# A hand-ordered attention and two feed-forward layers on one core: the order remade with VectorE and GpSimd taking turns, run on to unit fourteen, and constant matmuls ahead of the first load

## The chip, the cores and the metric

The kernel runs on one core of a Trainium2 chip. The metric is the device time of one execution in microseconds (us). The engines are TensorE (PE; its weight loads are PEld), VectorE (DVE), ScalarE (ACT), GpSimd (POOL) and SyncE (SP), on whose queue all the DMAs named below are issued.

## The reference

Three layers follow one another. All tensors are float32.

```python
# attention: q, k, v are (4, 8, 576, 64)
q_rot, k_rot = rotate(q), rotate(k)          # pairs (d, d+32) turned by position
scores = scale * q_rot @ k_rot^T
attn   = exp(scores - rowmax);  attn /= rowsum + 1e-9
x      = (attn @ v) -> (2304, 512)
# layer 2: w_in (512, 2048), w_out (2048, 512)
h = maximum(x @ w_in, 0);  x = h * h @ w_out
# layer 3: 8 experts, w1 (8, 512, 1024), w2 (8, 1024, 512)
e = argmax(x @ w_gate + modality_bias[modality_id])
out[t] = gate[t] * (maximum(x[t] @ w1[e], 0) @ w2[e])
```

## The kernel before

**Precision.** Matmul operands are split into a high part (rounded to the matmul's format) and a low part (the rest). A product is three passes: high by high, high by low, low by high.

**Attention** goes in 16 chunks of two heads. For a chunk, raw q and k (128 x 2 x 576: the values and their swapped partners) are loaded (`ldq`, `ldk`), multiplied by tables (`aq`, `bq`, `ak`, `bk`) and added (`cq`, `ck`; all L206). Then come the cast of the high part (`qh`, `kh`), the low part (`ql`, `kl0`, `kl1`; L195), and copies of both to the other partitions (`qd0` to `qd2`, `kd0` to `kd2`), by an engine or by DMA. There are nine groups of score rows; for each, matmuls into one of two PSUM buffers (`sc0` to `sc8`, L266), the maximum on VectorE (`mx`, L271), and the exponential on ScalarE, which also gives the row sums (`ex`, L282). TensorE transposes the exponentials (`trm..`, `trr.`; L324), an engine copies them out (`evm..`, `evr.`), and TensorE multiplies them by v (`pv0`, `pv1`). `sa` (the guard, L290) adds 1e-9 to the nine sums of a partition, `srec` takes the reciprocals, `sev` and `rst` send them to memory; `u0`, `u1` take the products out of PSUM. For the first four chunks `xn`, `xh`, `xl` normalise and split the result.

**The first block of layer 2.** A unit is one 128-wide slice f of the 2048 hidden columns for 512 tokens: `m1f` (12 matmuls of 512 columns, L649), `re`, `sq`, `gg`, `gl` (ScalarE and VectorE make the square and split it), `m2f` (12 matmuls of 512 columns, L685). Weights come as 32 chunks of 512 KB: `m1f` needs chunk 2f, `m2f` needs chunk 2f+1. A chunk goes through `wd` (load, into one of four raw buffers, L467), `wx` (ScalarE, L476 and L477), `wy` (VectorE, L481 and L482), `wz` (GpSimd, L486), `wb` (VectorE, L490; this frees the raw buffer), `wh` (ScalarE, L504) and `wl` (VectorE or GpSimd, L507). From chunk 10 on, `wh` needs memory that attention gives back. Later blocks of tokens use the converted weights again.

**The order** is written out: `ORDER` (L38) is a string of words `chunk.name.engine`, with V VectorE, A ScalarE, P GpSimd, T TensorE and D a DMA on SP's queue. Chunk 16 stands for the first block. The words are issued in this order; each engine runs its own in order, and semaphores keep what depends on one another. `HQ` (L436) is the number of units that are in `ORDER` whole. From unit `HQ` on a loop (L1087) issues the rest in program order: `m1` of two units ahead, what is listed for the unit (`at`, L1007), then `m2`. Before, with 12, the last words of the order make `m113` and `m211`, and the loop begins with `m114`, `m212`, `m115`, `m213`, `m116`. `m116` is the first of the next block of tokens and needs its x: `xk` and `xw` load reciprocals and values, `xnorm` multiplies, `xsplit` splits.

Of the kernel before, what the change touches and what calls it, by code (L numbers as in the profile page):

```python
# [43 lines left out]
1.kl0.P 0.trrk.T 0.ex8.A 0.evrk.V 0.evm02.V 1.kl1.P 1.sc1.T 1.sc3.T 0.evm00.A 0.evm03.A 1.mx1.V 1.ex1.A 1.mx3.V
0.trm13.T 1.ex3.A 0.sa.P 0.trm12.T 16.wx0.A 1.sc2.T 0.srec.V 0.evm13.V 0.evm12.V 0.trrr.T 0.trm11.T 1.mx2.V 2.ldq.D
1.ex2.A 1.sc0.T 1.qd2.D 0.trm10.T 1.sc6.T 0.evrr.A 1.mx0.V 2.ldk.D 1.ex0.A 0.evm11.A 1.sc5.T 2.aq.P 2.bq.P 0.trm01.T
1.trm02.T 2.cq.V 2.ak.V 2.bk.P 1.mx6.V 1.mx5.V 2.qh.A 0.sev.A 2.ck.V 2.ql.V 1.ex6.A 2.qd0.D 3.ldq.D 1.evm02.A
0.evm01.V 2.kh.A 1.ex5.A 2.kd1.A 1.trm03.T 1.sc8.T 2.kl0.P 1.mx8.V 2.kd0.V 1.ex8.A 2.qd1.D 0.trrq.T 0.evm10.V 0.evrq.A
2.kl1.P 1.trm00.T 1.sc4.T 1.sc7.T 1.mx7.V 2.kd2.D 0.rst.D 16.wy0.V 3.ldk.D 2.qd2.D 1.ex7.A 0.pv0.T 1.mx4.V 1.ex4.A
1.evm03.V 2.sc2.T 1.sa.V 2.mx2.V 3.aq.P 3.bq.P 1.srec.V 1.evm00.A 0.u0.A 2.ex2.A 1.trrq.T 2.sc1.T 3.cq.V 3.ak.V 3.bk.P  # L50
1.trm01.T 1.trm12.T 2.sc3.T 0.pv1.T 3.qh.A 1.evm01.A 2.mx1.V 2.mx3.V 3.ck.V 2.ex1.A 3.ql.V 2.ex3.A 0.rld.D 3.qd0.D
2.sc7.T 1.evrq.V 4.ldq.D 16.wz0.P 2.sc6.T 1.trm10.T 1.evm12.A 3.kh.A 1.trm11.T 3.kd1.A 2.mx7.V 2.mx6.V 3.kl0.P 2.ex7.A
2.sc4.T 1.trrr.T 2.ex6.A 3.kd0.V 2.sc0.T 3.qd1.D 1.evm11.A 0.u1.A 2.mx4.V 2.ex4.A 1.trm13.T 2.mx0.V 2.ex0.A 1.trrk.T
3.kl1.P 3.kd2.D 2.sc5.T 4.aq.V 1.evm10.A 2.sc8.T 1.evrr.A 2.mx5.V 0.xr.D 2.trm01.T 1.evm13.V 4.bq.P 2.mx8.V 3.qd2.D
1.sev.V 4.ldk.D 2.ex5.A 4.cq.P 2.evm01.A 2.ex8.A 3.sc2.T 2.trm13.T 3.mx2.V 4.qh.V 2.trm12.T 2.evm13.V 2.trm02.T
3.ex2.A 3.sc1.T 1.evrk.A 2.sa.P 2.evm02.A 3.sc3.T 3.mx1.V 4.qd0.D 2.trrq.T 2.trm11.T 3.mx3.V 2.trm00.T 3.ex1.A
2.evm12.V 2.evm11.V 4.ql.P 2.srec.V 2.ldv.D 4.bk.P 3.ex3.A 3.sc7.T 5.ldq.D 4.ak.P 2.trrk.T 3.sc6.T 2.evrq.A 2.trrr.T
3.mx7.V 16.wb0.V 4.ck.P 3.mx6.V 2.evrk.A 1.pv1.T 3.ex7.A 16.wx1.A 4.kh.V 2.evrr.V 3.sc4.T 3.ex6.A 1.u1.A 3.sc0.T
1.pv0.T 4.kd1.D 3.mx4.V 16.wx4.A 4.qd2.D 3.ex4.A 4.kd0.A 3.mx0.V 3.ex0.A 0.xn.P 4.kl0.V 3.sc5.T 5.aq.V 3.sc8.T 0.xh.A
4.kl1.V 3.mx5.V 1.u0.V 4.kd2.D 3.trm01.T 4.qd1.A 5.bq.P 3.mx8.V 2.trm10.T 5.ldk.D 3.ex5.A 2.sev.A 5.cq.P 2.evm00.V  # L60
3.evm01.A 3.ex8.A 2.evm10.A 4.sc3.T 2.trm03.T 3.trm13.T 5.qh.V 4.mx3.V 4.sc2.T 3.trm12.T 4.ex3.A 3.evm13.V 3.trm02.T
2.evm03.A 4.sc1.T 3.sa.P 3.evm02.A 1.rst.D 5.qd0.D 3.trrq.T 3.trm11.T 4.mx2.V 3.trm00.T 3.evm12.V 4.mx1.V 3.evm11.V
5.ql.P 3.srec.V 3.ldv.D 1.rld.D 5.bk.P 4.ex2.A 2.rst.D 6.ldq.D 5.ak.P 4.ex1.A 3.trrk.T 4.sc0.T 3.evrq.A 3.trrr.T
16.wy4.V 4.sc4.T 2.pv1.T 5.ck.P 4.mx0.V 4.mx4.V 4.ex0.A 3.evrk.A 4.ex4.A 5.kh.V 3.evrr.V 0.xl.V 5.kd1.D 0.xst.D
5.qd2.D 5.kd0.A 16.wh0.A 4.sc5.T 5.kl0.V 4.sc6.T 4.mx5.V 4.mx6.V 2.pv0.T 4.ex5.A 6.aq.V 5.kl1.V 4.ex6.A 5.kd2.D 2.u0.A
5.qd1.A 4.sc7.T 6.bq.P 4.ldv.D 3.trm10.T 6.ldk.D 1.xn.V 3.sev.A 6.cq.P 2.rld.D 4.sc8.T 3.evm00.V 4.mx7.V 2.u1.V
4.trm00.T 3.evm10.A 4.trm01.T 4.ex7.A 4.evm00.A 5.sc3.T 16.wy1.V 4.mx8.V 4.trm13.T 3.trm03.T 4.trm10.T 6.qh.V
4.evm01.A 16.wz4.P 4.trrk.T 5.mx3.V 4.ex8.A 5.sc2.T 4.evm13.V 5.ex3.A 3.evm03.A 4.trm12.T 4.evrk.A 5.sc1.T 4.trrq.T
4.trm11.T 6.qd0.D 4.evm10.V 5.mx2.V 4.sa.V 5.mx1.V 4.srec.V 4.trm03.T 6.ql.P 4.evm12.A 6.bk.P 4.trm02.T 5.ex2.A
4.evrq.A 3.rst.D 7.ldq.D 6.ak.P 5.ex1.A 4.evm02.A 4.evm11.V 4.trrr.T 5.sc0.T 1.xh.A 16.wd2.D 4.evm03.V 5.sc4.T 3.pv1.T  # L70
4.evrr.V 1.xl.V 6.ck.P 5.mx0.V 1.xst.D 5.mx4.V 16.wb4.V 5.ex0.A 16.wx2.A 5.ex4.A 6.kh.V 2.xn.V 4.sev.V 4.pv1.T 2.xr.D
2.xh.A 6.kd1.D 6.qd2.D 2.xl.V 6.kd0.A 5.sc5.T 6.kl0.V 5.sc6.T 5.mx5.V 5.mx6.V 2.xst.D 3.pv0.T 1.xr.D 5.ex5.A 4.pv0.T
7.aq.V 16.wy2.V 6.kl1.V 5.ex6.A 6.kd2.D 4.u1.A 3.u0.A 6.qd1.A 5.sc7.T 7.bq.P 5.ldv.D 4.rst.D 4.u0.A 7.ldk.D 7.cq.P
# [5 lines left out]
6.sc6.T 6.mx5.V 6.mx6.V 3.xst.D 6.ex5.A 5.pv0.T 8.aq.V 7.kl1.V 6.ex6.A 7.kd2.D 5.u1.A 7.qd1.A 6.sc7.T 8.bq.P 6.ldv.D
5.rst.D 5.u0.A 8.ldk.D 8.cq.P 6.sc8.T 6.mx7.V 6.trm00.T 16.wd3.D 5.xr.D 6.trm01.T 6.ex7.A 6.evm00.A 7.sc3.T 6.mx8.V  # L80
6.trm13.T 6.trm10.T 8.qh.V 6.evm01.A 6.trrk.T 7.mx3.V 6.ex8.A 7.sc2.T 6.evm13.V 7.ex3.A 6.trm12.T 6.evrk.A 7.sc1.T
6.trrq.T 6.trm11.T 8.qd0.D 6.evm10.V 7.mx2.V 6.sa.V 7.mx1.V 6.srec.V 6.trm03.T 8.ql.P 6.evm12.A 8.bk.P 6.trm02.T
7.ex2.A 6.evrq.A 9.ldq.D 8.ak.P 7.ex1.A 6.evm02.A 6.evm11.V 6.trrr.T 7.sc0.T 6.evm03.V 7.sc4.T 6.evrr.V 8.ck.P 7.mx0.V
7.mx4.V 7.ex0.A 7.ex4.A 16.wz2.P 8.kh.V 6.sev.V 6.pv1.T 8.kd1.D 16.wb2.V 8.qd2.D 8.kd0.A 7.sc5.T 8.kl0.V 7.sc6.T
7.mx5.V 7.mx6.V 16.wd5.D 7.ex5.A 6.pv0.T 9.aq.V 16.wx6.A 8.kl1.V 7.ex6.A 8.kd2.D 6.u1.A 8.qd1.A 7.sc7.T 9.bq.P
16.wy6.V 7.ldv.D 6.rst.D 6.u0.A 9.ldk.D 9.cq.P 7.sc8.T 7.mx7.V 7.trm00.T 6.xr.D 7.trm01.T 7.ex7.A 7.evm00.A 8.sc3.T
7.mx8.V 7.trm13.T 7.trm10.T 9.qh.V 7.evm01.A 7.trrk.T 8.mx3.V 7.ex8.A 8.sc2.T 7.evm13.V 8.ex3.A 7.trm12.T 7.evrk.A
8.sc1.T 7.trrq.T 7.trm11.T 9.qd0.D 7.evm10.V 8.mx2.V 7.sa.V 8.mx1.V 7.srec.V 7.trm03.T 9.ql.P 7.evm12.A 9.bk.P
7.trm02.T 16.wl4.P 8.ex2.A 7.evrq.A 10.ldq.D 9.ak.P 8.ex1.A 7.evm02.A 7.evm11.V 7.trrr.T 8.sc0.T 7.evm03.V 8.sc4.T
7.evrr.V 9.ck.P 8.mx0.V 8.mx4.V 8.ex0.A 8.ex4.A 9.kh.V 7.sev.V 7.pv1.T 16.wx5.A 9.kd1.D 9.qd2.D 9.kd0.A 16.wh2.A  # L90
8.sc5.T 9.kl0.V 8.sc6.T 8.mx5.V 8.mx6.V 8.ex5.A 7.pv0.T 10.aq.V 9.kl1.V 8.ex6.A 9.kd2.D 16.wy5.V 7.u1.A 9.qd1.A
8.sc7.T 10.bq.P 8.ldv.D 7.rst.D 7.u0.A 10.ldk.D 10.cq.P 8.sc8.T 8.mx7.V 8.trm00.T 7.xr.D 8.trm01.T 8.ex7.A 8.evm00.A
9.sc3.T 8.mx8.V 8.trm13.T 8.trm10.T 10.qh.V 8.evm01.A 8.trrk.T 9.mx3.V 8.ex8.A 9.sc2.T 8.evm13.V 9.ex3.A 8.trm12.T
# [1136 lines left out]
```

## Time and profile before

| | |
|---|---|
| median of 3 runs | 951.85 us (950.51 to 952.6) |
| profiled execution | 952.28 us, span 950.5 us |
| mean granted TensorE clock | 0.987 |
| TensorE busy | 894.2 us (94%) |
| VectorE, ScalarE, GpSimd busy | 649.4 (68%), 483.9 (51%), 263.1 (28%) |
| DMA | 117.28 MB, mean 123 GB/s |

The profiled execution's time is a little longer than its span, which goes from the first to the last instruction. Busy shares are means over stages of different kinds: attention ends near 299 us, the first block of layer 2 near 390 us, and what follows is mostly matmul. In the table of stretches below, the columns behind the length are PE, PEld, DVE, ACT and POOL (busy us and instructions), the granted TensorE clock, the DMA engines' busy share and GB/s; in the views of instructions, what stands in brackets is the engine's idle time before and what ended it.

### The profile page before, as it was taken

What the parts mean: (1) busy time and instruction counts of PE and PEld (TensorE: products, weight loads), DVE (VectorE), ACT (ScalarE), POOL (GpSimd) and SP (SyncE); (2) the same over time, 40 slices, a digit from 0 to 9 for tenths busy, and PEclk for the clock granted to TensorE, in tenths of its full rate; (3) what the DMA queues carried; (4) which work ended last, traced back from release to release, by engine and by line L of the source; (5) the groups of instructions that cost most, each with busy time, mean ns of one, the idle gap of its engine ahead of it and who ended that gap; (6) DMA issues with size and microseconds to landing.
All of it is one profiled execution on the core that took longest, in us unless ns stands there. A gap on an engine that the chain in (4) does not pass through costs nothing. (4 is left out here: it accounts for less than half of the span.)

```text
span 950.5 us, 14463 instructions
## 1 busy us (share of the span) xinstructions
PE 894.2 (94%) x5210; PEld 749.3 (79%) x5210; DVE 649.4 (68%) x1213; ACT 483.9 (51%) x956; POOL 263.1 (28%) x201
## 2 busy tenths in 40 slices
...
GB/s 230 136 129 159 175 207 146 154 164 156 190 125 204 122 128 83 163 123 12 1 54 80 1 1 72 17 1 1 45 200 45 111 214 269 227 215 237 204 101 35
DMA packets 47856, 117.28 MB, mean 123 GB/s; under 512 B 10448, under 2 KB 14560, under 8 KB 47776
## 3 DMA queue, kind: packets, MB, share of 16 engines
...
q14 instruction: 37, 0.30, 0.1%
HBM read 92.56 MB, written 15.54 MB: 114 GB/s over the span
## 5 line engine op out<-in xcount | busy, mean ns | idle before, releaser
L655 ACT ACTIVATE r<-h 128x512 f32<-128x512 f32 (+1 forms) x80 | 44.3, 554 | 230.8 <-PE h L649 214.8
L649 PE MATMUL h<-xs,w 128*128 128x512 f32 (+1 forms) x660 | 144.1, 368 | 1.2 <-DVE gl L667 1.2
L663 DVE SCALAR_TENSOR_TENSOR h<-h,r 128x512 f32<-128x512 f32 (+1 forms) x80 | 51.5, 643 | 124.9 <-ACT r L655 124.7
L685 PE MATMUL y<-w,gh 128*128 128x512 f32 x396 | 124.6, 396 | 11.1 <-ACT w L504 11.1
L649 PEld LDWEIGHTS h<-xs,w 128*128 128x128 f32 x660 | 115.8, 188 | 23.2 <-DVE gl L667 2.0
L282 ACT ACTIVATE e<-sc,nmx 128x576 f32<-128x576 f32 x144 | 106.4, 741 | 50.3 <-DVE nmx L271 48.9
L266 PE MATMUL sc<-kh,q 128*128 128x288 f32 (+1 forms) x336 | 100.0, 335 | 32.1 <-ACT e L282 18.7
L271 DVE TENSOR_REDUCE nmx<-sc 128x1 f32<-128x576 f32 x144 | 105.6, 752 | 17.8 <-PE sc L266 15.6
L266 PEld LDWEIGHTS sc<-kh,q 128*128 128x128 f32 x336 | 63.7, 199 | 52.5 <-ACT e L282 34.2
L923 DVE TENSOR_TENSOR w<-eraw,w 128x1024 fp32r<-128x1024 f32 x64 | 78.4, 1225 | 33.9 <-ACT w L922 33.5
L685 PEld LDWEIGHTS y<-w,gh 128*128 128x128 f32 x396 | 74.4, 191 | 26.6 <-ACT w L504 11.5
L266 PE MATMUL sc<-kl,q 128*128 128x288 f32 (+2 forms) x336 | 91.5, 308 | 0.0
L324 PE MATMUL b<-ident,e 128*128 128x128 f32 x640 | 82.9, 277 | 1.4 <-DVE et L192 0.8
L685 PE MATMUL y<-w,gl 128*128 128x512 f32 x198 | 78.0, 394 | 0.4 <-DVE gl L667 0.4
L969 PEld LDWEIGHTS h<-ye,w 128*128 128x128 f32 x576 | 74.0, 189 | 3.7
L324 PEld LDWEIGHTS b<-ident,e 128*128 128x128 f32 x640 | 74.4, 142 | 2.5 <-DVE et L192 1.1
L969 PE MATMUL h<-ye,w 128*128 128x256 f32 x576 | 74.8, 280 | 0.0
L992 PE MATMUL y<-w,ge 128*128 128x512 f32 x288 | 74.7, 395 | 0.0
L570 POOL TENSOR_TENSOR xraw<-xraw,rbs 128x512 f32<-128x512 f32 (+1 forms) x14 | 16.6, 1189 | 203.9 <-DMA rbs<-rD 189.6
L922 ACT ACTIVATE w<-eraw 128x1024 fp32r<-128x1024 f32 x64 | 67.3, 1052 | 4.1 <-DMA eraw<-wexp 4.1
L353 PE MATMUL b<-et,v 128*64 128x288 f32 x512 | 69.0, 412 | 0.0
L697 DVE SCALAR_TENSOR_TENSOR junk<-ysb,wgb 128x512 f32<-128x512 f32 x96 | 64.3, 725 | 0.0
(225 smaller groups left out, 1650.9 us busy)
## 6 DMA issues: line engine op xcount, KB each, us to landing
...
```

Source lines behind the costliest of these rows:

```text
L266: nc.tensor.matmul(out=o[:, x:x + w], lhsT=q[:, hd, q0:q0 + 128], rhs=k[:, hd, y:y + w], start=(n == 0), stop=(n == len(ops) - 1))
L271: nc.vector.tensor_reduce(out=m, in_=sc(p, j)[:, :, 0:HS], axis=AX.XY, op=ALU.max, negate=True)
L282: nc.scalar.activation(out=e(p)[:, o:o + S].rearrange("p (a b) -> p a b", a=2), in_=sc(p, j)[:, :, 0:HS], func=ACTF.Exp, bias=live[p, f"nm ...
L324: nc.tensor.transpose(t[:, i * 128:(i + 1) * 128], x[:, o:o + 128], ident)
L353: nc.tensor.matmul(out=o[64 * hd:64 * hd + 64], lhsT=lhsT, rhs=rhs, start=(c == 0), stop=(c == 4))
L649: nc.tensor.matmul(out=h, lhsT=w[:, a, k * 128:(k + 1) * 128], rhs=xs[b, k][:, c], start=(k == 0 and i == 0), stop=(k == 3 and i == 2))
L685: nc.tensor.matmul(out=yp[t], lhsT=g[a][:, t * 128:(t + 1) * 128], rhs=w[:, c, 512:1024], start=(begin and i == 0), stop=(f == NFC - 1 and ...
L697: nc.vector.scalar_tensor_tensor(out=junk, in0=ysb[j], scalar=1.0, in1=wgb[e], op0=ALU.mult, op1=ALU.mult, accum_out=lg[:, j, e:e + 1])
L922: nc.scalar.activation(out=w[:, 0], in_=r, func=ACTF.Copy)
L923: nc.vector.tensor_tensor(out=w[:, 1], in0=r, in1=f32(w[:, 0]), op=ALU.subtract)
L969: nc.tensor.matmul(out=h, lhsT=w[:, a, k * 128:(k + 1) * 128], rhs=x[:, c], start=(k == 0 and i == 0), stop=(k == 3 and i == 2))
L992: nc.tensor.matmul(out=yp[s, t], lhsT=g[a][:, t * 128:(t + 1) * 128], rhs=w[:, c, 512:1024], start=(f == 0 and i == 0), stop=(f == EFC - 1 ...
```

## The change

- `ORDER` is another string. It holds the same words for chunks 0 to 15, in another order and with other engines for many of them; the 16 guards, of which 13 were VectorE's, are all GpSimd's.
- `HQ` goes from 12 to 15. The order now holds `m114`, `m115`, `m116`, `m212`, `m213`, `m214` with their `re`, `sq`, `gg`, `gl`, the load `xw3`, the load of constants (`cl`), and the next block's normalising (`xo`, on GpSimd; before two of four on VectorE) and splitting (`xa`, `xb`) as words of their own.
- Before the first load is issued, VectorE fills 128 x 512 of a buffer of chunk 1 with ones, and TensorE is given 28 matmuls on it, 512 columns each, whose result the first score overwrites.

```diff
+WARM = 28
...
+        nc.vector.memset(f32(kh_buf[1][:, 0, 0:512]), 1.0)
+        o = sc(0, int(ORDER.split("0.sc")[1][0]))
+        for _ in range(WARM):
+            nc.tensor.matmul(out=o[:, 0], lhsT=kh_buf[1][:, 0, 0:128], rhs=kh_buf[1][:, 0, 0:512], start=True, stop=True)
         nc.sync.dma_start(out=tab["k"][LO], in_=tabs)
...
-HQ = 12
+HQ = 15
...
-        def xsplit(b, k):
-            x = raws.pop((b, k))
+        def xhigh(b, k):
+            x = raws[b, k]
...
+        def xlow(b, k):
+            t = xs[b, k]
+            nc.vector.tensor_tensor(out=t[:, 1], in0=raws.pop((b, k)), in1=f32(t[:, 0]), op=ALU.subtract)
...
-                        at(mid, q - 4, lambda b=b, k=k, e=e: xnorm(b, k, e))
...
-        at(mid, 13, cload)
...
+        yield dict(xk=lambda k: xrec(1, k), xw=lambda k: xraw(1, k), xo=lambda k, e: xnorm(1, k, e),
+                   xa=lambda k: xhigh(1, k), xb=lambda k: xlow(1, k), cl=lambda k: cload())
```

Of the order, first the words up to the first score, then those around the last four weight chunks:

```diff
-0.tab2.A 0.tab3.A 0.tab1.V 0.tab0.V 0.ak.V 0.bk.V 0.ck.V 0.aq.V 0.bq.V 0.cq.V 0.kh.A 0.qh.V 0.kd1.A 0.kd0.A 0.ql.V
-0.kd2.A 0.qd0.A 0.kl0.V 0.qd1.A 0.sc3.T 0.mx3.V 0.kl1.P 0.sc0.T 0.mx0.V 16.wd0.D 0.ex3.A 1.ldq.D 1.ldk.D 0.ex0.A
...
-16.wb29.V 16.wb19.V 16.wd25.D 16.wd30.D 16.gg11.V 16.wb23.V 16.wd27.D 16.sq11.A 16.wd31.D 16.wh19.A 16.re12.A
-16.re13.A 16.wh23.A 16.sq13.A 16.wh28.A 16.gl11.V 16.wl28.P 16.wl23.P 16.wl19.V 16.wx31.A 16.wh29.A 16.wx30.A
-16.wl29.P 16.wx25.A 16.wx27.A 16.gg13.V 16.wy27.V 16.wy31.V 16.m28.T 16.m29.T 16.wy30.V 16.gg12.V 16.wy25.V 16.gl13.V
-16.wz31.P 16.wz27.P 16.wz30.P 16.wz25.P 16.wb25.V 16.wb30.V 16.wb31.V 16.wb27.V 16.wh31.A 16.wh27.A 16.sq12.A
-16.wh25.A 16.wh30.A 16.wl25.V 16.wl27.V 16.gl12.V 16.wl30.V 16.wl31.V 16.xw1.D 16.xw2.D 16.xw0.D 16.xk2.D 16.xk3.D
-16.m211.T
...
+0.tab3.A 0.tab0.V 0.tab1.V 0.tab2.A 0.ak.V 0.bk.V 0.ck.V 0.aq.V 0.kh.A 0.bq.V 0.cq.V 0.qh.V 0.kd1.A 0.kd0.A 0.kd2.V
+0.qd0.A 0.ql.V 0.qd1.A 0.kl0.V 16.wd0.D 16.wd1.D 0.sc3.T 0.kl1.V 0.mx3.V 1.ldq.D 0.ldv.D 1.ldk.D 0.sc0.T 0.ex3.A
...
+16.gl6.V 16.wy29.V 16.wz23.P 16.wl28.P 16.wz29.P 16.m113.T 16.m26.T 16.m112.T 16.xk1.D 16.wd31.D 16.wd30.D 16.wb23.V
+16.gg11.V 16.wh19.A 16.sq11.A 16.gl8.V 16.wl19.V 16.wh23.A 16.wb29.V 16.gl11.V 16.wx30.A 16.wx31.A 16.wl23.P 16.wd25.D
+16.wd27.D 16.re13.A 16.wx25.A 16.wh29.A 16.re12.A 16.wy31.V 16.wy30.V 16.gg12.V 16.m211.T 16.m28.T 16.m114.T 16.m29.T
+16.wl29.V 16.wz31.P 16.wb31.V 16.wy25.V 16.wx27.A 16.sq13.A 16.wh31.A 16.wz30.P 16.wb30.V 16.sq12.A 16.wh30.A
+16.re14.A 16.wz25.P 16.wb25.V 16.sq14.A 16.wh25.A 16.wy27.V 16.wz27.P 16.gg13.V 16.gl12.V 16.wl30.V 16.gg14.V
+16.wb27.V 16.xw1.D 16.xk0.D 16.xw3.D 16.xw0.D 16.xw2.D 16.xo0.P 16.wl25.V 16.xo3.P 16.xo1.P 16.m115.T 16.re15.A
+16.xa0.A 16.wh27.A 16.gl14.V 16.sq15.A 16.xa1.A 16.gl13.V 16.gg15.V 16.wl27.V 16.wl31.V 16.xo2.P 16.xa2.A 16.m214.T
+16.m212.T 16.m213.T 16.xb1.V 16.cl0.D 16.xa3.A 16.xb3.V 16.xb2.V 16.gl15.V 16.xb0.V 16.m116.T 16.re16.A 16.gg16.V
+16.sq16.A 16.gl16.V
```

Words of chunks 0 to 15 and of the weights by engine, before and after (those that do not change are left out; a word of `ev` with `rq` or `rr` is two instructions):

```
aq V14 P2 -> V6 P10      bq V1 P15 -> V8 P8       ak V4 P12 -> V6 P10     bk V2 P14 -> V4 P12
ck V3 P13 -> V4 P12      cq V3 P13 -> V4 P12      kl V25 P7 -> V12 P20    ql V4 P12 -> V5 P11
kh V12 A4 -> V5 A11      qh V13 A3 -> V6 A10      sa V13 P3 -> V0 P16     sev V13 A3 -> V8 A8
evm V63 A65 -> V53 A75   evrk V1 A15 -> V3 A13    evrq V1 A15 -> V7 A9    evrr V14 A2 -> V11 A5
u V3 A29 -> V12 A20      xn V3 P1 -> V0 P4        xl V4 P0 -> V2 P2       wl V18 P14 -> V19 P13
kd V3 A19 D26 -> V10 A19 D19                      qd V2 A15 D31 -> V6 A11 D31
```

## Rows read from the trace of the kernel before

**Rows 1.** Table of stretches: start:end and length in us, each engine's busy us.

```profile
0.00:13.13 13.13, 0.00 (x1) 0.00 (x1) 9.00 (x21) 7.70 (x9) 4.15 (x9) 1.00 0.48 157
13.13:28.53 15.40, 13.08 (x52) 12.02 (x52) 11.24 (x15) 9.25 (x21) 6.11 (x5) 1.00 0.71 240
28.53:299.00 270.47, 252.24 (x1920) 200.07 (x1918) 246.16 (x395) 210.71 (x490) 153.18 (x107) 0.99 0.55 163
299.00:373.90 74.90, 73.94 (x324) 60.58 (x324) 53.48 (x82) 45.96 (x82) 30.04 (x23) 1.00 0.40 131
373.90:390.34 16.44, 4.91 (x10) 3.29 (x11) 13.81 (x19) 3.90 (x7) 8.46 (x6) 0.58 0.30 88
390.34:950.50 560.16, 550.07 (x2909) 473.36 (x2908) 315.75 (x683) 206.38 (x348) 61.13 (x53) 0.99 0.31 100
...
134.34:137.76 3.42, 3.42 (x16) 3.30 (x15) 1.96 (x3) 2.20 (x6) 1.86 (x1) 0.50 0.86 225
```

**Rows 2.** Waits from 28.53 to 299 us: total us, times, longest us.

```profile
ACT e L282 <- DVE nmx L271: 44.1, 40, 3.6
...
PE sc L266 <- ACT e L282: 16.4, 21, 2.4
```

**Rows 3.** Lines of VectorE, 28.53 to 299 us: busy us, mean ns, idle before.

```profile
L192 DVE COPY et<-b 128x512 f32<-128x512 f32 x63 | 40.4, 673 | 1.5 <-PE b L324 1.4
L195 DVE TENSOR_TENSOR kl<-rawk,kh 64x576 fp32r<-64x576 f32 x24 | 23.3, 970 | 0.4
...
L490 DVE SCALAR_TENSOR_TENSOR wmag<-wraw,wmag 128x512 int32<-128x512 int32 x12 | 11.3, 942 | 0.1
L192 DVE CAST kh<-rawk 128x576 fp32r<-128x576 f32 x12 | 9.9, 828 | 0.9 <-POOL rawk L206 0.9
L206 DVE TENSOR_TENSOR rawq<-rawq,tabq 128x576 f32<-128x576 f32 x12 | 9.0, 749 | 0.4 <-DMA rawq<-qx 0.4
...
L290 DVE TENSOR_SCALAR e<-e 128x9 f32<-128x9 f32 x13 | 7.4, 569 | 0.3 <-ACT e L282 0.3
L192 DVE CAST q<-rawq 128x576 fp32r<-128x576 f32 x12 | 6.3, 523 | 0.2
```

**Rows 4.** Lines of GpSimd in the same stretch.

```profile
L206 POOL TENSOR_TENSOR rawq<-rawq,tabq 128x576 f32<-128x576 f32 x16 | 25.2, 1581 | 3.7 <-DMA rawq<-qx 3.6
...
L195 POOL TENSOR_TENSOR kl<-rawk,kh 64x576 fp32r<-64x576 f32 x5 | 7.0, 1407 | 10.6 <-ACT kh L190 8.7 <-DVE kh L192 1.9
...
L290 POOL TENSOR_SCALAR e<-e 128x9 f32<-128x9 f32 x3 | 1.1, 350 | 3.7 <-ACT e L282 3.7
```

**Rows 5.** Instructions in order of time, first 40 us.

```profile
10.00 1.68 POOL L195 TENSOR_TENSOR kl<-rawk,kh 64x576 fp32r<-64x576 f32 x1 [6.85 <-DVE rawq L206]
10.45 1.84 DVE L195 TENSOR_TENSOR ql<-rawq,q 128x576 fp32r<-128x576 f32 x1
...
24.41 2.77 PE L324 MATMUL b<-ident,e 128*128 128x128 f32 x12
...
37.21 1.47 PE L324 MATMUL b<-ident,e 128*128 128x128 f32 x12
```

**Rows 6.** Instructions in order of time around the pause of the first block.

```profile
341.84 21.61 SPq L467 DMA_DIRECT2D wraw<-wio  x6
...
368.57 0.66 ACT L476 ACTIVATE wmag<-wraw 128x512 f32<-128x512 f32 x1 [3.31 <-DMA wraw<-wio]
...
385.02 1.52 PE L685 MATMUL y<-w,gh 128*128 128x512 f32 x2 [11.13 <-ACT w L504]
```

**Rows 7.** Instructions in order of time near 212 us: start, us, engine, operation.

```profile
211.78 1.99 DVE L490 SCALAR_TENSOR_TENSOR wmag<-wraw,wmag 128x512 int32<-128x512 int32 x1
211.78 1.44 POOL L206 TENSOR_TENSOR rawk<-rawk 128x576 f32<-128x576 f32 x1
...
213.70 1.41 DVE L271 TENSOR_REDUCE nmx<-sc 128x1 f32<-128x576 f32 x2
...
215.36 0.40 PE L266 MATMUL sc<-kh,q 128*128 128x288 f32 x1 [0.66 <-ACT e L282]
```

More of the change, by code (lines that the diff above doesn't have):

```diff
@@ L44 @@
[L44 to L73, printed above, removed]
@@ L79 @@
[L79 to L93, printed above, removed]
@@ new lines @@
+1.cq.P 0.ex4.A 0.mx1.V 0.ex1.A 1.qh.A 0.sc5.T 1.ak.V 1.bk.V 0.sc6.T 1.qd0.A 1.ck.P 0.mx5.V 0.mx6.V 1.ql.V 1.kh.V
+1.kl0.P 0.ex5.A 0.trm02.T 0.sc8.T 0.mx8.V 1.qd1.V 0.evm02.A 0.ex6.A 1.kd1.A 1.kd0.A 0.trm12.T 0.trm00.T 1.kd2.V
+0.ex8.A 0.trm03.T 1.qd2.A 0.evm00.A 0.evm03.A 0.trm11.T 1.kl1.V 1.sc1.T 1.ldv.D 2.ldq.D 2.ldk.D 1.sc3.T 0.trrk.T
+1.mx1.V 1.mx3.V 0.sa.P 0.trm13.T 2.aq.P 1.ex1.A 2.bq.P 1.ex3.A 2.ak.P 2.bk.P 0.evm12.V 1.sc2.T 0.evrk.V 0.evm13.A
+1.sc0.T 1.mx2.V 0.evm11.A 1.mx0.V 0.trm01.T 0.trm10.T 2.cq.V 0.trrq.T 0.srec.V 1.ex2.A 1.sc5.T 1.mx5.V 1.ex0.A
@@ new lines @@
+0.trrr.T 0.evm01.A 1.sc6.T 1.trm00.T 2.qh.A 1.ex5.A 0.evm10.A 2.ck.P 0.evrr.V 1.mx6.V 2.ql.V 0.sev.A 1.sc8.T 1.ex6.A
+0.evrq.V 1.sc4.T 1.mx8.V 2.kh.V 2.qd0.D 16.wd4.D 2.qd1.A 2.kd0.V 2.kl0.V 2.qd2.D 1.mx4.V 0.pv0.T 3.ldq.D 2.kd1.A
+1.evm00.V 1.ex8.A 2.kd2.A 1.ex4.A 1.trrq.T 1.sc7.T 16.wy0.V 0.u0.A 2.sc2.T 1.mx7.V 2.mx2.V 3.bq.V 3.aq.V 2.kl1.P
+0.pv1.T 2.ex2.A 3.cq.V 0.rst.D 3.ldk.D 1.ex7.A 1.sa.P 2.sc1.T 3.ak.P 2.sc3.T 2.mx1.V 1.evrq.A 1.trrk.T 1.trm03.T
+1.trm12.T 2.mx3.V 3.qh.A 0.u1.A 3.bk.V 2.ex1.A 3.qd0.D 3.ck.V 2.ex3.A 2.sc7.T 16.wd6.D 1.evm12.A 3.kh.A 2.sc6.T 3.ql.V
@@ new lines @@
+2.mx7.V 1.evm03.A 2.mx6.V 1.trm13.T 2.ex7.A 3.kl0.P 1.trm11.T 1.trm02.T 2.ex6.A 2.sc0.T 3.kd0.V 1.evm11.A 4.ldq.D
+1.evrk.A 3.kd1.D 2.sc4.T 2.mx0.V 2.ex0.A 2.mx4.V 3.qd1.D 1.srec.V 1.evm02.V 3.qd2.D 1.trm10.T 1.trm01.T 2.ex4.A
+2.sc5.T 2.mx5.V 3.kd2.V 2.trm01.T 1.evm10.A 1.evm13.A 2.sc8.T 2.evm01.V 16.wz0.P 2.ex5.A 0.rld.D 3.kl1.P 4.ldk.D
+2.trm02.T 1.evm01.A 2.mx8.V 3.sc2.T 1.trrr.T 2.evm02.A 3.mx2.V 2.ex8.A 1.evrr.V 1.sev.V 3.ex2.A 2.trm13.T 4.bq.P
+1.rst.D 2.trm12.T 4.aq.P 4.cq.P 3.sc1.T 2.trm11.T 4.qh.V 4.ql.P 3.mx1.V 3.sc3.T 2.evm13.A 2.evm11.A 2.trrk.T 3.mx3.V
```

186 lines of the change are left out of this document (105 added, 81 removed).

## The prediction

> **What bounds the kernel now.** I read the table of stretches first [rows 1], then the waits inside the attention stretch [rows 2], then the lines of VectorE and GpSimd there [rows 3, 4], and the instructions in order of time at the three places where TensorE stands still [rows 5, 6, 7].
>
> The stretches show a kernel that waits for TensorE nearly everywhere [rows 1]: from 390.34 us on it is busy for 550.07 of 560.16 us, and most of the missing ten lie behind its last matmul. The change puts no other instructions there. What can be won lies in front:
> - 0 to 13.13 us: TensorE does nothing; loads and the preparation of chunk 0.
> - 13.13 to 28.53: busy for 13.08 of 15.40, but slowly. The clock's record says 1.00 here; the matmuls say otherwise. [...]
> - 28.53 to 299.00 (attention): 252.24 busy of 270.47, so 18.2 idle. A stretch of 3.42 us at 134.34 ran at clock 0.50, which costs another 1.7. Together 19.9.
> - 299.00 to 373.90 (first block): 73.94 of 74.90. Its 324 matmuls of 512 columns give 73.94/324 = 0.228 us each; one unit of twelve takes 2.74.
> - 373.90 to 390.34: no matmul for 11.10 us, until 385.02 [rows 6], and then 4.91 us of work at half rate, which is 2.5 too much. With 0.4 of small gaps: 14.0.
>
> In attention, 16.4 of the 18.2 us are scores that wait for the exponential that empties their bank, and ScalarE has waited 44.1 us for the maxima of VectorE [rows 2]. VectorE is busy for 246.16 of 270.47 us: its queue is what everyone waits for, and 24.3 us of it are free.
>
> **The change, part by part.** The sum is made against the profiled execution, 952.28 us (span 950.5); the median of the runs shown is 951.85, so 0.4 comes off at the end.
>
> *First score.* Before, VectorE's low part of q takes 1.84 us at 10.45 because GpSimd runs at 10.00 for 1.68 us [rows 5]; without GpSimd beside it I take 0.75 for it (the price of another product of 128x576, [rows 3]). In the new order that GpSimd word (0.kl1) is VectorE's and comes after the first score, so 1.09 is won; but kd2 (64x576) goes to VectorE ahead of it, taken at 0.5 like the cast of q [rows 3]. Net -0.6. Bounds: -1.1 and 0.
>
> *Constant matmuls.* 28 of 512 columns, after one fill of 128x512 on VectorE (a fraction of the 4.1 us that VectorE has free in the first 13.13, [rows 1]). At full rate they take 28 x 0.228 = 6.4 us, at half rate 12.8. If they start by 1.5 and stay slow throughout, they end at 14.3 and the first score, then due at 12.5, is 1.8 late: against before +1.2. If they end early and the clock stays up, the 13.08 us of work shrink by 6.5 at most. But the scores there come in pairs of two banks, and maximum and exponential set their pace as soon as the matmuls are fast. So I take -2.5, nearer to the middle than to the end. The clock can also be lost between their end and the first score: in attention the 0.50 at 134.34 follows the longest pause there, 2.4 us [rows 1, 2]. Bounds -6.5 and +1.2.
>
> *Attention, remade.* I count words of both orders. Off VectorE go 13 low parts of k (0.970), 13 guards (0.569), 10 copies of transposes (0.673), 7 casts of k (0.828), 7 of q (0.523), 8 first products of q (0.749): 12.6 + 7.4 + 6.7 + 5.8 + 3.7 + 6.0 = 42.2 us [rows 3]. Onto it come 13 other products of the rotation at 0.749 = 9.7, and of the small words (moves, small copies, take-outs, normalising) 16 more than leave, at 0.523 = 8.4. Net -24.1 us of 246. GpSimd gets 13 low parts at 1.407 = 18.3 and 13 guards at 0.350 = 4.6, loses 5 products at 1.581 = 7.9, and gets 4 of about 1.407 = 5.6: +20.6 on 153.18 [rows 1, 4]. ScalarE's gains and losses are a few us on 210.71. Seven copies fewer are DMAs on SP's queue.
>
> VectorE's free time doubles, from 24 to 48 us, and I let the wait that hangs on its queue halve: 18.2/2 = -9. What is late next is TensorE itself, and GpSimd.
> Bounds: -19.9 (no idle, no lost clock) and +15 (the last rival).
>
> Against this speaks a row. At 211.78 a VectorE word and a GpSimd product start together; GpSimd's takes its 1.44 us, VectorE's 1.99, against 0.942 on average [rows 3]; the two maxima behind it start at 213.70, and TensorE then waits 0.66 for a score [rows 7]. So one GpSimd instruction can hold VectorE for its whole length, and 13 guards at 0.569 for 9 elements a lane on VectorE (0.350 on GpSimd) tell of the same [rows 3, 4]. If each new GpSimd microsecond held VectorE as long, 20.6 of the 24.1 would be taken back and attention would give 9 x 3.5/24.1 = -1.3.
> [...]
>
> *Guard on GpSimd* adds a wait: VectorE's reciprocal waits for it, behind that stand the next maxima, and for these ScalarE and TensorE. It is in the terms above at nothing, because the order has other VectorE words between the two; without that cover it is priced in the last rival.
>
> *Order run on to unit fourteen.* Before, units 12 to 14 followed in program order. TensorE wants weight chunk 25 after 27 units (27 x 2.74 = 74.0, at 373.90). But the last six loads are issued over 21.61 us, as raw buffers come free, ScalarE then waits 3.31 for the one that it takes first and that was issued last (31), and the last four (25, 30, 27, 31) are converted as one batch, from 368.57 to 385.02: 16.45 us [rows 6]. Now loads and conversions of these four stand in one sequence (31, 30, then 25, 27), and TensorE gets m115 (chunk 30) and m214 (29) before it wants 25 and 27. At the same pace, 16.45/4 = 4.1 each, they are ready at 372.7, 376.8, 380.9 and 385.0. Wanted: 30 at 373.9 (2.9 late), then 25 at 382.3 and 27 at 385.0 (in time). So 3 us remain, short enough for the clock to stay up: -14.0 + 3 = -11. The next block's x (loads, normalising, splitting) moves into the same queues; three units, 8.2 us of TensorE work, hide it. Without that cover it costs its chain of a few us. Bounds: -14.0, and 0 if chunk 30 is as late as before.
>
> Sum: -0.6 - 2.5 - 9 - 11 = -23.1, or 929.2; less 0.4, 929.
>
> **Rivals.**
> 1. *Forecast*, 929 (922 to 934). For it: each pause has a cause in the rows which an order can remove.
> 2. *GpSimd holds VectorE*: attention gives 1.3 instead of 9: 929 + 7.7 = 937. For it: [rows 7]; against: the two maxima of [rows 7] took 1.41 us together, beside a GpSimd product; work that reads PSUM is not held, and it is a large part of VectorE's.
> 3. *The stall of the first block stays*: chunk 30 or the next x is late, TensorE comes 12 us earlier and waits again: 952.3 - 12.1 - 0.4 = 940. For it: loads bound to free buffers; against: VectorE is busy for 53.48 of 74.90 us there, ScalarE and GpSimd for less [rows 1].
> 4. *TensorE never waits*: -1.1 - 6.5 - 19.9 - 14.0 = -41.5, or 911; as likely reached only half of the way from my forecast, 920. For it: nothing but order stands between; against: two banks of scores leave no slack.
> 5. *Slower*: GpSimd becomes the engine that all wait for. 13 reciprocals that each find the guard behind a product (1.581) and 13 low parts that each hold VectorE (1.407) cost 20.6 + 18.3 = 38.9 on VectorE, against 24.1 won: attention +15, and 929 + 9 + 15 = 953. Decides from some 38 us of such waits. Against: GpSimd is busy for only 153 of 270 us.
> 6. *It doesn't do what it says*: clock lost before the first score, pauses where they were: 951.
>
> **How the numbers follow.** Chances: 1: 0.47; 2: 0.20; 3: 0.13; 4: 0.11; 5: 0.06; 6: 0.03. The range goes from 911, the end of the fourth, to 943, a little above the third. No change means within 0.2% (1.9 us), about what a measurement can tell. Faster 0.91 (1 to 4), within 0.2% 0.03 (6), slower 0.06 (5).
>
> **What would show it.** First score near 12.5 us. Transposes before 28 us at some 0.12 us each. TensorE idle for about 9 us between 28 us and the end of attention, VectorE busy for some 220 there, kl on GpSimd near 1.4 us. No pause over 3 us before 390 and no clock of 0.50 there. Wrong it is if TensorE's waits for exponentials stay at 16 us, if a new wait for GpSimd stands among VectorE's, or if a pause of the old length opens in front of m115 or m116.

## The result, and the profile after

The changed kernel takes 926.79 us (median of 4, 926.34 to 927.68), the kernel before 952.23 beside it: ratio 0.9737, 95% interval 0.9721 to 0.9754. Measured again, beside the first experiments, it was 924.82, ratio 0.9699 (0.9678 to 0.9719). The forecast was 929 us.

The table of stretches of the changed kernel, cut at the first score, near the end of the half rate, at the first matmul of layer 2, and behind `m116`, past the place where the first block paused before; the columns are those of [rows 1]:

```profile
0.00:12.86 12.86, 8.58 (x28) 6.60 (x29) 8.96 (x24) 7.03 (x8) 2.48 (x8) 0.98 0.61 201
12.86:26.04 13.18, 10.85 (x39) 9.41 (x40) 9.97 (x15) 9.03 (x20) 4.36 (x3) 0.50 0.42 139
26.04:288.78 262.74, 253.74 (x1930) 201.44 (x1929) 221.50 (x369) 215.05 (x497) 172.37 (x131) 1.00 0.57 168
288.78:376.50 87.72, 87.72 (x387) 72.42 (x387) 75.25 (x109) 55.08 (x99) 46.85 (x33) 1.00 0.50 152
376.50:924.50 548.00, 537.90 (x2858) 463.54 (x2856) 310.83 (x673) 202.85 (x342) 60.96 (x53) 0.99 0.31 99
```

The third row is attention: TensorE stands for 9.0 of 262.74 us (before 18.2 of 270.47), VectorE is busy for 221.50 (246.16), GpSimd for 172.37 (153.18). The fourth is the first block: no gap at all. Two landmarks split the gain. The first matmul of layer 2 comes at 288.78 in place of 298.91 (10.1 earlier), the first output copy of the first block at 380.25 in place of 406.08 (25.8 earlier); from there to the end nothing more comes. So 10.1 lie in the start and attention, 15.7 in the first block.

Waits of the changed kernel from 26.04 to 288.78 us (total us, times, longest us), against [rows 2]:

```profile
ACT e L286 <- DVE nmx L275: 30.0, 33, 2.8
POOL e L294 <- ACT e L286: 27.3, 8, 10.7
DVE nmx L275 <- PE sc L270: 20.1, 32, 2.5
...
PE sc L270 <- ACT e L286: 4.3, 11, 0.9
```

TensorE's waits for exponentials fell from 16.4 to 4.3 us, ScalarE's for maxima from 44.1 to 30.0. New is the second line: GpSimd stands for the last exponential in front of its guards. Half of VectorE's idle time, 20.1 of 41.2 us, is spent waiting for TensorE's scores (third line), the same share as before (11.8 of 24.3).

Lines of VectorE, then of GpSimd, in the same stretch (busy us, mean ns, idle before), against [rows 3, 4]:

```profile
L196 DVE COPY et<-b 128x512 f32<-128x512 f32 x53 | 35.5, 682 | 2.3 <-PE b L328 1.8
L210 DVE TENSOR_TENSOR rawq<-rawq,tabq 128x576 f32<-128x576 f32 x11 | 10.1, 927 | 1.9 <-DMA rawq<-qx 1.8
L498 DVE SCALAR_TENSOR_TENSOR wmag<-wraw,wmag 128x512 int32<-128x512 int32 x12 | 9.7, 810 | 1.5 <-POOL wmag L494 1.5
L199 DVE TENSOR_TENSOR kl<-rawk,kh 64x576 fp32r<-64x576 f32 x10 | 9.4, 940 | 0.2
...
L297 DVE RECIPROCAL e<-e 128x9 f32<-128x9 f32 x16 | 3.3, 208 | 0.1
```

```profile
L199 POOL TENSOR_TENSOR kl<-rawk,kh 64x576 fp32r<-64x576 f32 x20 | 30.7, 1533 | 16.9 <-ACT kh L194 7.5 <-DVE kh L196 5.8 <-DMA kh<-kh 3.1
...
L294 POOL TENSOR_SCALAR e<-e 128x9 f32<-128x9 f32 x16 | 6.2, 385 | 29.1 <-ACT e L286 27.3 <-DMA xT<-xo 1.3
```

The first 16 us of TensorE (start, us, operation, count, idle before):

```profile
1.45 8.58 PE L414 MATMUL sc<-kh 128*128 128x512 f32 x28 [1.45 <-DVE kh L411]
12.86 0.61 PE L270 MATMUL sc<-kh,q 128*128 128x288 f32 x1 [2.83 <-ACT q L194]
13.27 0.44 PE L270 MATMUL sc<-kl,q 128*128 128x288 f32 x1
13.51 0.44 PE L270 MATMUL sc<-kh,q 128*128 128x288 f32 x1
```

The constant matmuls end at 10.03; TensorE then waits 2.83 us for q. In this trace the granted clock is recorded at 0.50 from 12.45 to 26.10 us, and the scores start 0.24 us apart, as slowly as without any constant matmul. In the second trace of the same kernel the pause is 2.36 us; the first scores start 0.13 us apart, and from 13.79 on, 0.76 us after the first, 0.24.

The end of the weights' conversion, against [rows 6]: SP's last loads; ScalarE's first steps of chunk 30 and of chunk 27; VectorE's last step of chunk 30 and those of 27 and 31; `m115`, which needs chunk 30:

```profile
341.49 9.64 SPq L475 DMA_DIRECT2D wraw<-wio  x4
```

```profile
347.81 0.66 ACT L484 ACTIVATE wmag<-wraw 128x512 f32<-128x512 f32 x1
...
356.00 0.69 ACT L484 ACTIVATE wmag<-wraw 128x512 f32<-128x512 f32 x1 [2.92 <-DVE w L515]
```

```profile
361.72 0.89 DVE L515 TENSOR_TENSOR w<-wmag,w 128x512 fp32r<-128x512 f32 x1
...
367.02 3.30 DVE L515 TENSOR_TENSOR w<-wmag,w 128x512 fp32r<-128x512 f32 x2 [0.34 <-ACT w L512]
```

```profile
362.40 2.92 PE L660 MATMUL h<-xs,w 128*128 128x512 f32 x12
```

In the kernel before, VectorE's last steps of chunks 30 and 31:

```profile
386.81 3.41 DVE L507 TENSOR_TENSOR w<-wmag,w 128x512 fp32r<-128x512 f32 x2
```

Layer 2 itself begins 10.1 us earlier, so times are best counted from its first matmul (288.78, before 298.91). The last load is issued by 62.4 us in place of 64.5, only 2 earlier; ScalarE's first step of the last four chunks starts at 59.0 in place of 69.7 (368.57 in [rows 6]), and their last part is ready at 81.5 (370.32) in place of 91.3 (390.22).

### The profile page after: what moved, and what is told of

The parts are those of the page before. It is cut to its first block, busy times and chain, and to the rows that moved or that the text cites. A ratio compares the mean times of both kernels' runs of the same rounds, so it can differ in the third digit from the quotient of the medians.

```text
span 924.5 us, 14559 instructions
## 1 busy us (share of the span) xinstructions
PE 898.8 (97%) x5238; PEld 753.4 (81%) x5238; DVE 626.5 (68%) x1187; ACT 489.0 (53%) x964; POOL 287.0 (31%) x227
## 5 line engine op out<-in xcount | busy, mean ns | idle before, releaser
L286 ACT ACTIVATE e<-sc,nmx 128x576 f32<-128x576 f32 x144 | 106.5, 742 | 35.2 <-DVE nmx L275 33.7
L696 PE MATMUL y<-w,gh 128*128 128x512 f32 x396 | 122.7, 391 | 0.0
L578 POOL TENSOR_TENSOR xraw<-xraw,rbs 128x512 f32<-128x512 f32 (+1 forms) x16 | 19.5, 1228 | 193.8 <-DMA rbs<-rD 187.3
```

The costliest lines, as they stand in the source:

```text
L286: nc.scalar.activation(out=e(p)[:, o:o + S].rearrange("p (a b) -> p a b", a=2), in_=sc(p, j)[:, :, 0:HS], func=ACTF.Exp, bias=live[p, f"nm ...
L696: nc.tensor.matmul(out=yp[t], lhsT=g[a][:, t * 128:(t + 1) * 128], rhs=w[:, c, 512:1024], start=(begin and i == 0), stop=(f == NFC - 1 and ...
```

## The experiments

Times are medians; ratios are to the kernel before, with the 95% interval.

### The start: are the constant matmuls worth anything?

Theory 1: a clock that stays up shortens the first 13 us of matmuls. Theory 2: maximum and exponential set the pace there, and the clock is worth nothing. Three kernels, measured on one chip.

The changed kernel once more:

> The changed kernel once more, to stand beside the three others of this group on one chip: 926.8 us within 1. Both theories say the same of it.

Measured: 924.82 us, 0.9699 (0.9678 to 0.9719).

Without fill and constant matmuls:

```diff
-        nc.vector.memset(f32(kh_buf[1][:, 0, 0:512]), 1.0)
-        o = sc(0, int(ORDER.split("0.sc")[1][0]))
-        for _ in range(WARM):
-            nc.tensor.matmul(out=o[:, 0], ...)
```

> The fill and the 28 constant matmuls are taken out; all else is the changed kernel. Theory 1 (the clock they raise at 5.6 us is lost again at 12.4, ahead of the first score at 12.9, so they give nothing): 926.8 within 1.5, the first 39 or so real matmuls at half rate as in the changed kernel. Theory 2 (they win part of the way, say by an earlier second rise of the clock): 2 to 3 us slower, 929 to 930.

Measured: 925.92 us, 0.9722 (0.9703 to 0.974). First score at 12.49.

Forty of them:

```diff
-WARM = 28
+WARM = 40
```

> 40 constant matmuls in place of 28. The 28 ended at 10.0 us; 12 more at 0.22 us end near 12.7, about when the first score is due. Theory 1 (only the 2.8 us of pause lost the clock): no clock of 0.50 between 12 and 26 us, scores 0.13 us apart instead of 0.24, and 2 to 4 us off: 923 to 925. Theory 2 (the pairs of scores are paced by maximum and exponential, so a fast clock only makes TensorE wait longer): clock at 1.00, but time within 1 us of the changed kernel. If the clock falls again among the first scores, whose pauses are long at the full rate, the time also stays.

Measured: 924.27 us, 0.9689 (0.9671 to 0.9708). TensorE's first instructions in this trace, and its clock (columns of [rows 1]):

```profile
1.46 11.31 PE L414 MATMUL sc<-kh 128*128 128x512 f32 x40 [1.46 <-DVE kh L411]
12.67 0.40 PE L270 MATMUL sc<-kh,q 128*128 128x288 f32 x1
12.90 0.30 PE L270 MATMUL sc<-kl,q 128*128 128x288 f32 x1
13.04 0.30 PE L270 MATMUL sc<-kh,q 128*128 128x288 f32 x1
```

```profile
5.60:26.04 20.44, 16.31 (x93) 13.40 (x92) 18.14 (x29) 15.68 (x31) 5.65 (x4) 1.00 0.56 192
```

Here no gap lies before the first score and the clock stays at 1.00, with scores 0.13 to 0.14 us apart. TensorE waits longer for exponentials up to 26.04 us (4.1 us, with 28 constant matmuls 2.3). The first sixteen transposes in a row start at 24.48 (26.93 with 28, 26.66 without any), 2.4 us ahead; at the first matmul of layer 2 the lead is 1.2 (287.59 beside 288.78), less than two traces of different executions can settle: without any constant matmul it came at 286.08. The medians, 925.92, 924.82 and 924.27, lie closer together than the executions of one kernel (922.5 to 927.6 with 28). Theory 2 fits: the constant matmuls as they stand gain nothing that is measured, and a held clock at most some 2 us by the medians.

### Where the gain lies

The changed order up to its first matmul of the first block (`16.m14`), then the words of the old one, with `HQ` 12 and the old code behind it; and the reverse. The constant matmuls stand in both, and a few words at the seam change places:

```diff
-ORDER = <after>
+ORDER = <after up to 16.m14.T> + <words of before that are left>
```

> The new order up to the first matmul of layer 2, constant matmuls included, and from there the words of the order of before, run on only to unit eleven. Theory 1 (the gains stand in different places and add: 10 us in attention, 16 in the first block): 942 us (940 to 944), the pause of 11 us in front of the second product of unit twelve is there again, with its clock of 0.50. Theory 2 (the first block runs well because attention hands over more converted weights): 930 to 936.

Measured: 945.28 us, 0.9915 (0.9894 to 0.9936).

```diff
-ORDER = <after>
+ORDER = <before up to 16.m14.T> + <words of after that are left>
```

> The order of before up to the first matmul of layer 2, and from there the new one with three more units; the constant matmuls stay. Theory 1 (the gains add): 937 us (935 to 939), no pause in the first block. Theory 2 (the new tail needs the new attention's state of the weights): a pause of some us stays, 940 to 946.

Measured: 935.74 us, 0.981 (0.9792 to 0.9827). TensorE's waits over the whole span, the first splice, then the second:

```profile
PE y L690 <- ACT w L509: 11.3, 1, 11.3
PE sc L267 <- ACT e L283: 5.8, 11, 1.2
PE h L654 <- DVE gl L672: 5.8, 3, 3.0
```

```profile
PE sc L269 <- ACT e L285: 17.7, 23, 2.2
```

Each half brings back the wait of its own old half: the pause of 11.3 us with the old tail, 17.7 us of waits for exponentials with the old attention. Against 953.63 beside them, the tail alone wins 17.9 us, attention alone 8.4 (the seam takes some back: the 5.8 us for `gl` stand in neither whole kernel). The two add up to the gain within a few us. 945.28 lies just above what was expected if they add (940 to 944), 935.74 inside it (935 to 939).

### Order or engines?

Theory 1: what counts in attention is VectorE's load. Theory 2: order and engines must fit. The order of before with the engine letters of after (228 words), and the changed order with the letters of before:

```diff
-4.aq.V ... 4.sa.V
+4.aq.P ... 4.sa.P
```

> The kernel before, its words in their order, but each word of chunks 0 to 15 on the engine that the new order gives it (228 words move). Theory 1 (attention was bound by VectorE's load, so taking 24 us off it is the gain): 942 to 946 us. Theory 2 (the sequence is the gain, load without fitting turns is worth nothing): within 3 us of before or slower, 950 to 965, with more of TensorE's idle time in attention, because words then stand where their new engine is not free.

Measured: 974.82 us, 1.0242 (1.0204 to 1.0279).

```diff
-4.aq.P ... 4.sa.P
+4.aq.V ... 4.sa.V
```

> The changed kernel, its words in their new order, but each word of chunks 0 to 15 on the engine that the order of before gave it. Theory 1 (load is the gain): attention loses its 10 us again, 935 to 939. Theory 2 (the sequence is the gain): much of it stays, 927 to 932. If both matter and fit each other, it is slower than 939.

Measured: 980.97 us, 1.0301 (1.0271 to 1.0331). Waits from 26 to 300 us (attention ends at 321 and 342 us here), the old order with new engines, then the reverse:

```profile
ACT e L282 <- DVE nmx L271: 48.7, 35, 5.4
...
PE sc L266 <- ACT e L282: 25.9, 24, 3.9
```

```profile
ACT e L286 <- DVE nmx L275: 65.0, 46, 7.1
...
PE sc L270 <- ACT e L286: 27.0, 26, 6.3
```

Each alone is worse than the kernel before, by 21 and 27 us, the second although it has the new tail; 974.82 lies above what either theory allowed. ScalarE waits longer for maxima (48.7 us) than before (44.1, [rows 2]). But the first run does not test a lighter VectorE, because VectorE is hardly lighter in it. From the end of the half rate to layer 2, old order with new engines:

```profile
26.30:320.96 294.66, 260.89 (x1930) 204.47 (x1928) 242.13 (x369) 216.62 (x503) 176.03 (x134) 0.98 0.49 147
```

VectorE's 369 instructions are busy for 242.13 us, the 369 of the changed kernel for 221.50, the 395 of the kernel before for 246.16. The traces show what the order does here. From the first score to layer 2, 39 of VectorE's instructions in the kernel before took over 0.15 us longer than their kind does at its fastest, 33.7 us together; with the new engines in the old order 39, 36.4 us; in the changed kernel 26, 17.0 us (second trace: 28, 20.1). Each of them, in every trace, started while a GpSimd instruction ran. So the new order takes a good part of the time away for which GpSimd holds VectorE, and the new engines alone do not; how much of the run time that is worth was not run by itself.

### What a microsecond of VectorE costs in the changed order

The 13 guards back on VectorE, at their places; then each moved to just in front of its reciprocal; then, with the guards on GpSimd, the 16 low parts of k that were moved there back on VectorE:

```diff
-4.sa.P 5.sc3.T 5.mx3.V 4.srec.V
+4.sa.V 5.sc3.T 5.mx3.V 4.srec.V
```

> 13 of the 16 guards go back from GpSimd to VectorE, as they were before; order and all else as in the changed kernel. Theory 1 (VectorE's queue is what attention waits for, and a guard there is held by GpSimd): 13 x 0.57 = 7.4 us more on VectorE, of which half reach TensorE's waits at most: 0 to 4 us slower, 927 to 931. Theory 2 (the guard on GpSimd makes VectorE's reciprocal wait behind long GpSimd products): 1 to 3 us faster, 924 to 926.

Measured: 935.12 us, 0.9806 (0.9788 to 0.9824).

```diff
-4.sa.P 5.sc3.T 5.mx3.V 4.srec.V
+5.sc3.T 5.mx3.V 4.sa.V 4.srec.V
```

> The changed kernel with the 13 guards on VectorE again, each now moved back in VectorE's order to the place just in front of its reciprocal, where before they stood earlier and VectorE stood for the last exponential. Guards on VectorE at their places in the changed order cost 10 us (935.1 beside 924.8), with 7.6 us held and 3.9 us stood in front of them. If the standing is what costs (VectorE in order, everything behind it late), it goes with this move and the time is 925 to 929. If the held 7.6 us cost, by VectorE's share of the chain from maximum to exponential, it stays near 930 to 934.

Measured: 934.63 us, 0.9821 (0.9802 to 0.9841).

```diff
-4.kl1.P
+4.kl1.V
```

> The changed kernel with the 16 low parts of keys that it moved to GpSimd back on VectorE (0.94 us each there, 15 us in all; GpSimd loses 25 us of 172). If each us of load on VectorE is a us of time, as with the guards, 937 to 941. If half the load shows, as the forecast had it, 932. If VectorE's idle time (41 us of 263 in the attention) takes it, 925 to 928.

Measured: 934.94 us, 0.983 (0.9808 to 0.9851). The guards' line on VectorE in the first and in the second kernel, and the low parts' in the third:

```profile
L294 DVE TENSOR_SCALAR e<-e 128x9 f32<-128x9 f32 x13 | 7.6, 587 | 3.9 <-ACT e L286 3.9
```

```profile
L294 DVE TENSOR_SCALAR e<-e 128x9 f32<-128x9 f32 x13 | 9.3, 718 | 0.1
```

```profile
L199 DVE TENSOR_TENSOR kl<-rawk,kh 64x576 fp32r<-64x576 f32 x26 | 25.7, 988 | 1.3 <-ACT kh L194 0.7
```

Beside the changed kernel on its own chip the first costs 10.3 us. The other two ran on a chip without it; by their ratios to the kernel before (0.9821 and 0.983, the changed kernel 0.9737 and 0.9699) they cost 8 to 12.5. Moving the guard takes its wait away (3.9 to 0.1) but makes it longer (7.6 to 9.3), and the time stays: 11.5 us of VectorE, then 9.4, for about 10. That is more than either theory of the first run allowed (931 at most). The low parts add 15.9 us to their line and, with other lines shorter, 11.3 to 15.4 to VectorE's busy time (641.9 beside 630.6 and 626.5 in the two profiles of the changed kernel); their 934.94 lies between what was expected if half of it shows (932) and if all does (937 to 941). So in this order a us of guards on VectorE costs about a us, whether it is work or standing, and a us of low parts between half and all of one; that VectorE's idle 41 us take it is refuted. The reading (argued, not run): half of that idle time is spent waiting for scores, and work placed elsewhere in the order cannot fill it.

### The guard alone, in the old order

The kernel before with its 13 guards on GpSimd, nothing else:

```diff
-5.sa.V 6.mx1.V 5.srec.V 5.trm03.T 7.ql.P
+5.sa.P 6.mx1.V 5.srec.V 5.trm03.T 7.ql.P
```

> The kernel before with one edit: its 13 guards of VectorE run on GpSimd (GpSimd's order, which has room: 153 of 270 us busy in that stretch), nothing else. If a guard on VectorE costs its length wherever the order puts it, this gains what it cost in the changed order, 7 to 10 us: 942 to 945. If it was the changed order that could not carry it (it has GpSimd wait 27 us for the last exponential at these instructions), and the order of before, which has its guards at places where VectorE waits only 0.3 us, hides them or makes GpSimd's loads late instead, the time is 949 to 956.

Measured: 963.84 us, 1.0123 (1.0102 to 1.0144): slower by 11.7 us, outside both expectations. GpSimd's instructions in order of time around one guard:

```profile
155.25 1.92 POOL L206 TENSOR_TENSOR rawq<-rawq 128x576 f32<-128x576 f32 x1 [3.47 <-DVE rawq L206]
161.22 0.24 POOL L290 TENSOR_SCALAR e<-e 128x9 f32<-128x9 f32 x1 [4.06 <-ACT e L282]
161.54 1.43 POOL L195 TENSOR_TENSOR ql<-rawq,q 128x576 fp32r<-128x576 f32 x1
162.92 1.42 POOL L206 TENSOR_TENSOR rawk<-rawk,tabk 128x576 f32<-128x576 f32 x1
...
173.38 1.93 POOL L206 TENSOR_TENSOR rawq<-rawq 128x576 f32<-128x576 f32 x1 [3.56 <-DVE rawq L206]
```

The guard takes 0.24 us and stands for 4.06; the low part of q and the rotary products of the next chunks stand behind it. A chunk takes 18.1 us (155.25 to 173.38), in the kernel before 16.6 (150.99 to 167.58). All guards together stood for 48.5 us. The next run takes the cause away: in 10 chunks that low part goes ahead of the guard.

```diff
-5.sa.P 6.mx1.V 5.srec.V 5.trm03.T 7.ql.P
+7.ql.P 5.sa.P 6.mx1.V 5.srec.V 5.trm03.T
```

> The order of before with its 13 guards on GpSimd, as in the run where that alone cost 11.7 us (963.8 beside 952.2), and in 10 of the units GpSimd's next low part of queries moved in front of the guard instead of behind it. In that run GpSimd stood 48.5 us for the last exponential at its guards (15 times, longest 9.9), the low part started right behind it and four rotary products behind that, and one unit took 17.7 to 18.1 us in place of 16.5 to 16.6. If what costs is that these instructions stand behind the waiting guard, the move gives most of it back: 951 to 955, and below 949 if VectorE's relief of 7 us then shows. If it is the reciprocal on VectorE that comes late after a hop to another engine, the time stays at 962 to 968, since the guard comes no sooner.

Measured: 955.33 us, 1.0027 (1.0013 to 1.0041). GpSimd again, in this kernel:

```profile
151.53 1.91 POOL L206 TENSOR_TENSOR rawq<-rawq 128x576 f32<-128x576 f32 x1 [3.48 <-DVE rawq L206]
156.02 1.43 POOL L195 TENSOR_TENSOR ql<-rawq,q 128x576 fp32r<-128x576 f32 x1 [2.58 <-ACT e L282]
157.53 0.24 POOL L290 TENSOR_SCALAR e<-e 128x9 f32<-128x9 f32 x1
157.85 1.43 POOL L206 TENSOR_TENSOR rawk<-rawk,tabk 128x576 f32<-128x576 f32 x1
...
168.32 1.94 POOL L206 TENSOR_TENSOR rawq<-rawq 128x576 f32<-128x576 f32 x1 [3.56 <-DVE rawq L206]
```

This guard waits for nothing now (15.6 us of standing are left at all guards), a chunk takes 16.8 us, and the kernel is 2.5 us slower than the one before beside it (952.81) in place of 11.7: some 9 us are back. The guard itself runs no sooner in its chunk (6.0 us after the chunk's first row in both views), so what cost was not a late reciprocal but what stood behind the waiting guard. The guards' 7 us that VectorE no longer has win nothing here. In the two traces GpSimd runs guard and low part as the words stand: the low part of q starts 0.32 us after the guard in one (161.22, 161.54), and 1.51 ahead of it in the other (156.02, 157.53).

## Why the prediction was right, and where not

The time (929 forecast, 926.79) came out well inside the range, but so close in part by luck: two of its terms were missed with opposite signs. Against its profiled execution, 952.28, the changed kernel's was 926.34: -25.9, forecast -23.1.

- *First score*, -0.6: it came 0.27 earlier (13.13 to 12.86). It lay anywhere from 12.44 to 13.03 in other runs with this start, so the term is too small to be settled. Its parts came as forecast (the low part of q took 0.76 us in place of 1.84, kd2 0.45), but VectorE's work began 0.34 later, when the tables had landed (5.05 beside 4.71).
- *Constant matmuls*, -2.5: not borne out. The step "So I take -2.5, nearer to the middle" lets the clock stay up half of the way; the two sentences around it were nearer to what came: the clock was lost behind the 2.83 us between their end and the first score, and where it was held (forty) half of the lead was gone by the end of attention, as TensorE waited longer for exponentials. Worth by the medians: 1.1 us (925.92 to 924.82), within the scatter. The bound of -6.5 takes the 13.08 us of work at half rate. In the kernel before, scores there start 0.24 us apart (13.53, 13.77), later ones 0.13 (56.93, 57.06), and twelve transposes take 2.77 us at 24.41, 1.47 at 37.21 [rows 5].
- *Attention*, -9: from first score to layer 2 it took 9.86 us less, with the constant matmuls' share in it. VectorE's load fell by 24.7 us (forecast 24.1), GpSimd's rose by 19.2 (20.6), TensorE stands for 9.0 us (9). The size was right, the reason only in part: the count prices the words that move at the means of before, whatever the order, and "VectorE's free time doubles, and I let the wait halve" takes load as the cause. The same engines in the old order brought 4.0 of the 24 us (246.16 to 242.13) and cost 21 us more than before. Some 14 to 17 us of the fall are instructions that GpSimd holds no longer (33.7 to 17.0, or 20.1), and that is the order's doing. What was won is a sequence that fits the engines; that the fall in held time by itself brings the 9 us is not shown.
- *Guard on GpSimd*, at nothing: the cover that I named is there (the reciprocal's line shows 0.1 us of idle). But I listed only what stands behind the reciprocal on VectorE, not what stands behind the guard on GpSimd, where 27.3 us of standing arose. What they cost in the changed order was not run (GpSimd has 90 us free there, and TensorE has no wait for it); in the old one, where the guard alone moved, they cost most of 11.7.
- *First block*, -11: it was -15.7, beyond my own bound of -14.0, which left out the 0.96 us of gaps before 373.90 in [rows 1]. The failed step is "at the same pace, 16.45/4 = 4.1 each". It lets the four chunks start where they started before, at 368.57, and takes 385.02 for the batch's end, where it was only the high part of chunk 25 that had come; the last part came at 390.22. Counted from the first matmul of layer 2, ScalarE took up the first of the four 10.6 us sooner, and chunk 30 was ready at 73.8 us (362.61), in the forecast at 77.9 (376.8); `m115` started at 73.6 and waited for nothing. The forecast's 3 us of rest do not exist. Which part of the new tail made the room, the earlier loads or the place of the conversions, was not run apart. That a rest of 3 us is "short enough for the clock to stay up" no run shows either: behind pauses of 2.36 and 2.83 us the clock fell (scores 0.24 us apart, with forty constant matmuls and no pause 0.13 to 0.14).

Of the rivals, GpSimd holding VectorE is refuted for the changed order, where the held time fell; it is what happened in the old order with the new engines, where VectorE's load fell by 4.0 us and the rival has 3.5. Single lines got longer (the product of the rotation 749 to 927 ns) and others shorter (the sign step 942 to 810). GpSimd did become an engine with long waits, as in the slower rival, but in front of the guard, not of the reciprocal. The rival in which TensorE never waits adds up to 910, not 911. Behind the first score no pause over 3 us is left before 390 us; a clock of 0.50 there is, from 12.45 to 26.10.
